# A gMLP block with one gelu per row tile, norms in place in three groups, a padded output projection, and outputs three tiles behind the gates

## The chip, the cores and the metric

The kernel runs on one core of a Trainium2 chip. The metric is the device time of one execution in microseconds (us), lower is better. TensorE is PE here, VectorE DVE, ScalarE ACT, GpSimd POOL, SyncE SP. SP, ACT and POOL also issue DMA transfers, each from its own queue, in the order of its instructions.

## The reference

Two layers run twice: a recurrent memory attention (A) and a gMLP (B), each behind a layer norm and a residual. Only B is changed. S is 2048 rows, D 512, F 1376, Fh 688.

```python
def _B_ref(x, w_in, w_sp, b_sp, w_out):
    z = _gelu(jnp.einsum('bsd,df->bsf', x, w_in))
    z1 = z[..., :Fh].copy()
    z2 = _layernorm(z[..., Fh:], axis=-1)
    g = jnp.einsum('ts,bsf->btf', w_sp, z2) + b_sp[None, :, None]
    return jnp.einsum('bsf,fd->bsd', z1 * g, w_out)
x = x + _A_ref(_layernorm(x, axis=-1), A_mem0, A_Wq, A_Wk, A_Wv, A_Wo, A_seg_len)
x = x + _B_ref(_layernorm(x, axis=-1), B_w_in, B_w_sp, B_b_sp, B_w_out)
```

The last two lines stand twice in the reference. Every gate row needs all 2048 rows of the normalised z2, so all of the projection comes before the first complete gate.

## The kernel before, in words

The program is A, B, A, B in time; the two B parts are called block 0 and block 1. A runs 64 segments of 32 rows, one after the other, and is not touched except in two places named below.

B (`b_block`, from line 227) works on 16 row tiles of 128 rows, in three stages.

**Projection.** `project` (line 261) takes the transposed input rows of one tile, runs twelve matmuls into `pz` (three PSUM banks, two buffers), then two gelus on ACT: the half to be normalised goes to an f32 tile `z2` (four buffers), the other half to `z1` in bf16. DVE takes statistics of `z2` (lines 273 to 275). After every second tile `norms` (line 277) computes the reciprocal roots of the two tiles on DVE, a chain of twelve small instructions in `_rstd_dve`, and ACT writes the normalised tiles to `z2n` (line 290), one pair behind the projection. The input rows come through `load_rows` (line 159), a DMA transpose on SP of two tiles at a time.

The last four row tiles of A (12 to 15) are not summed and normalised when B begins. `late_load` (line 253) loads their residual rows and A's output, POOL adds them (line 213) and stores them to `xd`; their statistics and norms go with the groups of tiles 5 and 7 on DVE (line 223), POOL stores the result to `xb_d`, and SP's transposes for tiles 12 to 15 read it. Their buffers are borrowed: one is a buffer of the spatial weights (`wspL`).

**Gates.** For each output tile t, `gate` runs 32 matmuls over the 16 source tiles into `pg`; `product` (line 335) adds the bias and multiplies by `z1` on DVE into `u`, whose 688 columns are padded to 768 by zeros; a DMA transpose on SP turns `u` into `uT`. The spatial weights `wspT` have three buffers: `product(t)` issues the load of t + 3, ahead of the transpose of `u` on SP's queue, and it waits until gate t has read its buffer.

**Outputs.** `finish` (line 357) runs six matmuls against `w_out`, in chunks of 128 rows and one of 48 (`FCH`), adds the residual on DVE into `xo` (one buffer), and stores it. In block 0 the statistics and reciprocal root of the output rows follow on DVE and ACT, for the next A. `finish(t - 2)` stands in the middle of gate t; the last tile is turned by PE and ACT (`turn_u`, line 349).

PE, DVE, ACT and, in B, SP run in the order of the code (`manual_schedule`, line 241); POOL's order is chosen by the framework. PE's order at the end of B is:

```python
for t in range(2, NT):
    gate(t, range(0, 10))
    finish(t - 2)
    gate(t, range(10, NT))
    product(t)
finish(NT - 2)
turn_u(NT - 1)
finish(NT - 1)
```

In A, `pads_of` splits some matmuls of a segment in two, so that each segment holds a whole number of pages of 256 PE instructions; `FILL_AHEAD` tells it how many stand before the first segment.

Of the kernel before, what the change touches and what calls it, by code (L numbers as in the profile page):

```python
# [14 lines left out]
P = 128  # L15
DM = 512
# [12 lines left out]
FILL_AHEAD = ((0, 0, 0, 106), (0, 0, 0, 94))  # L29
FCH = [(0, 128), (128, 128), (256, 128), (384, 128), (512, 128), (640, 48)]  # L30
# [137 lines left out]
class _Rows:  # L168
# [33 lines left out]
    def y_load(self, tb, first, eng, x=None, o=None):  # L202
        if x is None:
            x = self.pool.tile([P, DM], F32, name="y_x")[:]
            o = self.pool.tile([P, DM], F32, name="y_o")[:]
        x = x[:, 0:DM // 2].bitcast(BF16) if first else x
        eng.dma_start(x, (self.x_in if first else self.xd)[tb * P:(tb + 1) * P, :])
        eng.dma_start(o, self.o_d[M + tb * P:M + (tb + 1) * P, :])
        self.y[tb] = (o, x)

# [8 lines left out]
    def y_norm(self, tb, mean, rstd, store):  # L219

        o, _ = self.y.pop(tb)
        xn = self.pool.tile([P, DM], BF16, name="ln_xn", bufs=2)
        self.nc.vector.tensor_scalar(out=_nat(xn[:]), in0=_perm(o), scalar1=mean, scalar2=rstd, op0=ALU.subtract, op1=ALU.mult)
        store.dma_start(self.xb_d[tb * P:(tb + 1) * P, :], xn[:])


def b_block(tc, c, rows, front, xd, MV_out, RS_out, w_sp, w_out, S, first, out_final=None):
# [4 lines left out]
    with ExitStack() as ctx:  # L232
        mid = ctx.enter_context(tc.tile_pool(name="b_mid", bufs=1))
# [4 lines left out]
        ps_pool = ctx.enter_context(tc.tile_pool(name="b_ps", bufs=1, space=PSUM))  # L238
        big = _Tagged(ps_pool, "big", 2)
        one = _Tagged(ps_pool, "one", 2)  # L240
        ctx.enter_context(tc.manual_schedule(engines=ORDERED | {mybir.EngineType.SP}))

        w_in_sb = front.w_in_sb
        z1 = mid.tile([P, NT, FH], BF16, name="z1")
        z2n = mid.tile([P, NT, FH], BF16, name="z2n")
        w_out_sb = mid.tile([P, 6, DM], BF16, name="w_out_sb")
        xt, z2, wsp, mv, rs, nb = {}, {}, {}, {}, {}, {}
# [5 lines left out]
        def late_load(tb, x=None, o=None):  # L253
            rows.y_load(tb, first, nc.gpsimd, x=x, o=o)
            rows.y_add(tb, first, nc.gpsimd, nc.gpsimd)

        def load_wsp(t):
            wsp[t] = wsp_pool.tile([P, NT, P], BF16, name="wspT", tag="wspT")
            nc.sync.dma_start_transpose(out=wsp[t][:], in_=w_sp[t * P:(t + 1) * P, :].rearrange("t (st s) -> t st s", s=P))

        def project(tt):
            pz = big.tile([P, 1536], F32, name="pz")
            xnT = front.xnT[tt // 2][:, :, P * (tt % 2):P * (tt % 2) + P]
            for c0, c1 in ((0, 512), (512, 1024), (1024, FF)):
                for kt in range(KT):
                    nc.tensor.matmul(pz[:, c0:c1], lhsT=xnT[:, kt, :], rhs=w_in_sb[:, kt, c0:c1], start=(kt == 0), stop=(kt == KT - 1))  # L266
            z2[tt] = zp.tile([P, FH], F32, name="z2", bufs=4)
            nc.scalar.activation(out=z2[tt][:], in_=pz[:, 0:FH], func=ACT.Gelu_apprx_tanh)
            nc.scalar.activation(out=z1[:, tt, :], in_=pz[:, FH:FF], func=ACT.Gelu_apprx_tanh)
            if tt % 2 == 0:  # L270
                mv[tt // 2] = zp.tile([P, 4, 2], F32, name="mv")
            st = zp.tile([P, 2, nc.vector.BN_STATS_DIM], F32, name="bnst2")
            nc.vector.bn_stats(out=st[:, 0, :], in_=z2[tt][:, 0:344])
            nc.vector.bn_stats(out=st[:, 1, :], in_=z2[tt][:, 344:FH])
            nc.vector.bn_aggr(out=mv[tt // 2][:, tt % 2, :], in_=st[:])

        def norms(q, late):

            n = 4 if late else 2
            for k, tb in enumerate(late):  # L280
                rows.y_stats(tb, mv[q][:, 2 + k, :])
            rs[q] = zp.tile([P, 4], F32, name="rs")
            nb[q] = zp.tile([P, 2], F32, name="nb")
            _rstd_dve(nc, zp, rs[q][:, 0:n], mv[q][:, 0:n, 1], n)
            nc.vector.scalar_tensor_tensor(out=nb[q][:], in0=mv[q][:, 0:2, 0], scalar=-1.0, in1=rs[q][:, 0:2], op0=ALU.mult, op1=ALU.mult)
            for k, tb in enumerate(late):
                rows.y_norm(tb, mv[q][:, 2 + k, 0:1], rs[q][:, 2 + k:3 + k], nc.gpsimd)

        def normalise(tt):
            nc.scalar.activation(out=z2n[:, tt, :], in_=z2.pop(tt)[:], func=ACT.Identity, bias=nb[tt // 2][:, tt % 2:tt % 2 + 1],  # L290
                                 scale=rs[tt // 2][:, tt % 2:tt % 2 + 1])

        nc.gpsimd.dma_start(w_out_sb[:, 0:5, :], w_out[0:640, :].rearrange("(fc p) d -> p fc d", p=P))
        nc.gpsimd.dma_start(w_out_sb[0:48, 5, :], w_out[640:688, :])
        late_load(NT - 4)
        late_load(NT - 3, gp.tile([P, DM], F32, name="xs", bufs=3)[:], gp.tile([P, DM], F32, name="xo", bufs=1)[:])
        late_load(NT - 2, *(gp.tile([P, DM], F32, name="xs", bufs=3)[:] for _ in range(2)))
        wl = wsp_pool.tile([P, 2, DM], F32, name="wspL", tag="wspT")
        late_load(NT - 1, wl[:, 0, :], wl[:, 1, :])
        for tt in range(NT):  # L300
            project(tt)
            if tt in (7, 9, 11):
                load_wsp((tt - 7) // 2)
            if tt == 14:
                load_x(0)
            if tt % 2 == 1:
                if tt // 2 + 3 < NT // 2:
                    front.load_rows(tt // 2 + 3)
                norms(tt // 2, {5: (NT - 4, NT - 3), 7: (NT - 2, NT - 1)}.get(tt, ()))
                if tt > 1:  # L310
                    normalise(tt - 3)
                    normalise(tt - 2)
        normalise(NT - 2)
        normalise(NT - 1)

        zctx.close()
        up = ctx.enter_context(tc.tile_pool(name="b_u", bufs=2))

# [8 lines left out]
        def gate(t, sts):  # L327
            if sts[0] == 0:
                pg[t] = big.tile([P, 3, 512], F32, name="pg")
            for st in sts:  # L330
                for k in range(2):
                    nc.tensor.matmul(pg[t][:, k, 0:344], lhsT=wsp[t][:, st, :], rhs=z2n[:, st, 344 * k:344 * k + 344],  # L332
                                     start=(st == 0), stop=(st == NT - 1))

        def product(t):
            del wsp[t]
            if t + 3 < NT:
                load_wsp(t + 3)
            u[t] = us[t % 2]
            nc.vector.scalar_tensor_tensor(out=u[t][:, 0:FH].rearrange("p (k f) -> p k f", k=2), in0=pg.pop(t)[:, 0:2, 0:344],  # L340
                                           scalar=c["bsp"][:, t:t + 1], in1=z1[:, t, :].rearrange("p (k f) -> p k f", k=2),
                                           op0=ALU.add, op1=ALU.mult)
            if t + 1 < NT:
                load_x(t + 1)

                uT[t] = up.tile([P, 6, P], BF16, name="uT")
                nc.sync.dma_start_transpose(out=uT[t][:], in_=u[t][:].rearrange("t (fc s) -> t fc s", s=P))

        def turn_u(t):
            pT = one.tile([P, 1024], BF16, name="pT")  # L350
            for fc, (f0, fsz) in enumerate(FCH):
                nc.tensor.transpose(pT[0:fsz, fc * P:(fc + 1) * P], u[t][:, f0:f0 + fsz], ident_bf[:])
            uT[t] = up.tile([P, 6, P], BF16, name="uT")
            nc.scalar.copy(uT[t][:, 0:5, :].rearrange("p fc r -> p (fc r)"), pT[:, 0:640])
            nc.scalar.copy(uT[t][0:48, 5, :], pT[0:48, 640:768])

        def finish(t):
            py = one.tile([P, DM], F32, name="py")
            for fc, (f0, fsz) in enumerate(FCH):
                nc.tensor.matmul(py[:], lhsT=uT[t][0:fsz, fc, :], rhs=w_out_sb[0:fsz, fc, :], start=(fc == 0), stop=(fc == 5))  # L360
# [16 lines left out]
        gate(0, range(0, NT - 2))  # L377
        gate(1, range(0, NT - 2))
        gate(0, range(NT - 2, NT))
        product(0)  # L380
        gate(1, range(NT - 2, NT))
        product(1)
        for t in range(2, NT):
            gate(t, range(0, 10))
            finish(t - 2)
            gate(t, range(10, NT))
            product(t)
        finish(NT - 2)
        turn_u(NT - 1)
# [89 lines left out]
def a_block(tc, c, rows, front, MV_in, RS_in, MV_out, RS_out, wqkv, Wo, S, first):  # L479
# [6 lines left out]
    with ExitStack() as ctx:  # L486
# [383 lines left out]
        for s in range(NSEG):  # L870
# [21 lines left out]
            def tail():  # L892
# [11 lines left out]
                if due and (j4 != 3 or tb + 2 >= NB):  # L904
                    ys.append(due.pop(0))
                    rows.y_load(ys[0], first, nc.sync)
# [51 lines left out]
```

## Time and profile before

| what | us |
|---|---|
| median of 3 runs (1819.06 to 1823.71) | 1821.11 |
| the profiled execution, its own time | 1841.74 |
| its span on the core | 1840.0 |
| PE busy, of the span | 1729.5 (94%) |
| PE's weight loads | 1277.5 (69%) |
| DVE busy | 1172.4 (64%) |
| ACT busy | 1130.6 (61%) |
| POOL busy | 136.6 (7%) |
| block 0: first projection matmul to last output matmul | 776.87 to about 933.4 |
| block 1: the same | 1683.36 to about 1836.5 |

Times below are from the start of the profiled execution's span. The profiled execution is 20.6 us longer than the median of the plain runs, so differences are taken within it and then carried over to the median. A row of the timeline gives the start, the length, the engine, the line, the operation, output and inputs, shapes, and in brackets the idle time before it with what ended that. PE is matmuls, PEld the weight loads that run beside them; SPq, ACTq and POOLq are DMA instructions on those engines' queues.

### The profile page before, as it was taken

The page shows a single profiled execution, that of the slowest core. Times are in us where ns is not written, and L with a number is a line of the kernel's source. Part 1 is how long each engine was busy: PE and PEld are TensorE (multiplying, and loading weights), DVE is VectorE, ACT ScalarE, POOL GpSimd, SP SyncE. Part 2 cuts the span into 40 slices and gives each one's busy share as a digit, 9 for nine tenths or more (in the row PEclk, how much of TensorE's full clock was granted, in tenths as well). Part 3 has the DMA queues.
Part 4 walks back from the last instruction along what each step waited for, and adds up shares of the span by engine and source line. Part 5 has one row for each costly group of instructions (what it writes and reads, how often), then busy time and mean ns, then how long its engine had stood idle before and what let it go on. Part 6 is the DMA issues. An engine that isn't in the chain of part 4 may idle for free.

```text
span 1840.0 us, 109962 instructions
## 1 busy us (share of the span) xinstructions
PE 1729.5 (94%) x51154; PEld 1277.5 (69%) x51178; DVE 1172.4 (64%) x2956; ACT 1130.6 (61%) x2330; POOL 136.6 (7%) x289
## 2 busy tenths in 40 slices
PE   2999999999999999888979999999999999998898
PEld 1777777777777777645547777777777777775455
DVE  1666666677767766583446666666766776665622
ACT  1777777777777777571037777777777777765500
POOL 5000000000000000122010000000000000003000
PEclk8999999999999999999989999999999999999999
DMA  9100000021002112359840000001200120125576
GB/s 347 56 23 19 18 23 19 19 80 34 21 25 81 35 30 42 92 141 191 192 126 22 22 22 23 22 22 45 82 27 23 48 86 26 36 62 153 114 172 132
DMA packets 189331, 126.81 MB, mean 69 GB/s; under 512 B 135896, under 2 KB 164328, under 8 KB 188872
## 3 DMA queue, kind: packets, MB, share of 16 engines
q1 hardware_dynamic: 167016, 71.01, 16.7%
q0 software_dynamic: 10560, 34.07, 5.6%
q10 hardware_dynamic: 11296, 14.70, 2.7%
q8 instruction: 400, 6.55, 1.5%
q14 instruction: 59, 0.48, 0.1%
HBM read 59.29 MB, written 33.56 MB: 50 GB/s over the span
## 4 chain that ended last, share of the span: by engine, by line
PE 87%; issue 4%; DMA 3%; DVE 3%; ACT 1%; POOL 1%; SPq 0%; ACTq 0%; POOLq 0%; DVEq 0%
PE psm L544 13%; PE pw L602 13%; PE psV L544 13%; PE psm L719 12%; PE psb L544 10%; PE pg L332 8%; PE psS L743 4%; PE psO L769 4%; PE pwB L616 3%; PE py L360 3%; PE psD L824 2%; PE psM L815 1%; PE pz L266 1%; DMA Wo_sb<-in_A_Wo_dram 1%; DMA uT<-u 1%
## 5 line engine op out<-in xcount | busy, mean ns | idle before, releaser
L544 PEld LDWEIGHTS <-hA 128*32 128x32 bf16 x11102 | 361.5, 96 | 165.2 <-DVE hA L660 53.4
L544 PE MATMUL psV<-Wv_sb,hA 128*32 128x256 bf16 (+1 forms) x5880 | 288.1, 315 | 0.6 <-issue 0.2
L602 PE MATMUL pw<-Wo_sb,uT 128*32 128x128 bf16 x16640 | 269.6, 220 | 14.8 <-issue 8.1
L602 PEld LDWEIGHTS <-uT 128*32 128x32 bf16 x16640 | 238.6, 97 | 61.6 <-DVE uT L836 42.5
L706 ACT CAST rows<-psm 128x512 bf16<-128x512 f32 x256 | 149.8, 585 | 146.8 <-PE psm L544 146.8
L719 PEld LDWEIGHTS <-hA 128*32 128x32 bf16 x8192 | 237.8, 97 | 1.3 <-issue 0.5
L783 DVE TENSOR_TENSOR uT<-psO,Rt 128x384 bf16<-128x384 f32 x256 | 140.7, 550 | 100.5 <-ACT Rt L842 100.5
L722 ACT CAST rows<-psm 128x256 bf16<-128x256 f32 x512 | 191.2, 374 | 17.6 <-PE psm L719 0.3
L750 ACT ACTIVATE E<-psS 128x448 bf16<-128x448 f32 x256 | 126.3, 541 | 117.2 <-PE psS L743 117.2
L836 DVE TENSOR_TENSOR uT<-psO,Rm 128x128 bf16<-128x128 f32 x256 | 62.5, 286 | 174.8 <-PE psO L769 174.8
L544 PE MATMUL psm<-Wk_sb,hA 128*32 128x256 bf16 (+1 forms) x3158 | 151.9, 308 | 10.3 <-issue 8.9
L842 ACT ACTIVATE Rt<-Rt 128x512 f32<-128x512 f32 x256 | 157.4, 629 | 4.0
L332 PE MATMUL pg<-z2n,wspT 128*128 128x344 bf16 x1024 | 156.4, 311 | 1.0 <-DVE u L340 1.0
L544 PE MATMUL psm<-Wq_sb,hA 128*32 128x512 bf16 x2064 | 135.8, 384 | 10.2 <-DVE hA L660 8.8
L719 PE MATMUL psm<-Wq_sb,hA 128*32 128x256 bf16 x4096 | 138.5, 273 | 0.0
L719 PE MATMUL psm<-Wk_sb,hA 128*32 128x256 bf16 x4096 | 138.0, 273 | 0.0
L332 PEld LDWEIGHTS <-wspT 128*128 128x128 bf16 x1024 | 98.4, 98 | 55.6 <-issue 8.2
L544 PEld LDWEIGHTS <-hB 128*32 128x32 bf16 x3072 | 91.8, 98 | 62.7 <-DVE hB L559 25.3
L753 DVE TENSOR_TENSOR E<-E,maskN 128x448 bf16<-128x448 bf16 x256 | 104.2, 408 | 39.3 <-ACT E L750 37.7
L834 ACT ACTIVATE Rt<-psD 128x1024 f32<-128x1024 f32 x128 | 128.8, 1006 | 0.0
L710 DVE STREAM_TRANSPOSE QQ<-rows 128x512 bf16<-128x512 bf16 x128 | 88.9, 695 | 45.5 <-ACT rows L706 45.5
L710 DVE STREAM_TRANSPOSE KA<-rows 128x512 bf16<-128x512 bf16 x128 | 90.6, 708 | 38.3 <-ACT rows L706 37.8
(151 smaller groups left out, 2690.6 us busy)
## 6 DMA issues: line engine op xcount, KB each, us to landing
Wo_sb<-in_A_Wo_dram POOLq DMA_DIRECT2D x8, 1024.0 KB, 13.3
xs<-xd ACTq DMA_DIRECT2D x32, 256.0 KB
o_d<-o_sb SPq DMA_DIRECT2D x126, 64.0 KB
y_o<-o_d SPq DMA_DIRECT2D x24, 256.0 KB
xd<-y_o SPq DMA_DIRECT2D x22, 256.0 KB
Wq_sb<-in_A_Wq_dram POOLq DMA_DIRECT2D x8, 512.0 KB, 7.8
Wk_sb<-in_A_Wk_dram POOLq DMA_DIRECT2D x8, 512.0 KB, 11.1
Wv_sb<-in_A_Wv_dram POOLq DMA_DIRECT2D x8, 512.0 KB, 10.9
```

The lines of the kernel that those rows point to most:

```text
L332: nc.tensor.matmul(pg[t][:, k, 0:344], lhsT=wsp[t][:, st, :], rhs=z2n[:, st, 344 * k:344 * k + 344], start=(st == 0), stop=(st == NT - 1))
L544: nc.tensor.matmul(o, lhsT=lhs(kt, cg), rhs=r, start=(kt == 0 and a == 0), stop=(kt == KT - 1 or halved > 0), tile_position=(0, 32 * cg), ...
L602: nc.tensor.matmul(po[32 * cg:32 * cg + 32, 0:128], lhsT=lhs[:, n, :], rhs=wo_rhs(h, cg), start=(h == 0), stop=(h == H - 1), tile_position ...
L706: nc.scalar.copy(r[:], ps[:])
L710: nc.vector.transpose(out=QQ[:, j % 2, :, 0:32] if j < 2 else KA[:, j % 2], in_=r[:])
L719: nc.tensor.matmul(ps[32 * cg:32 * cg + 32, 0:256].rearrange("p (i c) -> p i c", i=2), lhsT=hA_cur[:, kt, :], rhs=qk_rhs(j, kt, cg)[:, 2 * ...
L722: nc.scalar.copy(r[:, 256 * a:256 * a + 256], ps[:, 0:256])
L750: nc.scalar.activation(out=E[:, r], in_=pS, func=ACT.Exp, scale=scale)
L753: nc.vector.tensor_tensor(out=E[:, r], in0=E[:, r], in1=maskN[:, j4, :].unsqueeze(1).to_broadcast([P, 4, 112]), op=ALU.mult)
L783: nc.vector.tensor_tensor(out=hview(uT_nxt[:], r, 8, 32), in0=oview(r, 8, 32), in1=r_view(r)[:, :, :, 0:24], op=ALU.mult)
L834: nc.scalar.activation(out=Rt[:], in_=psD[:], func=ACT.Ln)
L842: nc.scalar.activation(out=rt, in_=rt, func=ACT.Exp, scale=-1.0)
```

## The change

One gelu per tile writes all 1376 columns in bf16 to one array z, which is split in two tiles of 9 and 7 row tiles; `z1`, `z2` and `z2n` go. Statistics are taken from the bf16 values. The norms overwrite z in place, in three groups (0 to 3 with the four late rows, 4 to 9, 10 to 15): tiles 0 to 5 on ACT behind the gelus of 10 to 15, tiles 6 to 9 and 10 to 15 on DVE. The late rows are summed on DVE after tile 3; two of their norms stay on DVE, two go to ACT after tile 8. `w_out` is zero-padded, and the six chunks are all 128 rows. The code loads `w_out` at tile 11, and the third `w_sp` at tile 10 rather than 11. In the gate stage PSUM holds three gates of two banks each; the first ten source tiles of three gates run first, and outputs stand three tiles behind. Residual rows are loaded later. `y_load` returns the second load as a function to be called.

```diff
-FILL_AHEAD = ((0, 0, 0, 106), (0, 0, 0, 94))
-FCH = [(0, 128), (128, 128), (256, 128), (384, 128), (512, 128), (640, 48)]
+FILL_AHEAD = ((0, 0, 0, 106), (0, 0, 0, 88))
...
-    def y_norm(self, tb, mean, rstd, store):
+    def y_norm(self, tb, mean, rstd, store, shift=None):
...
+        if shift is not None:
+            self.nc.scalar.activation(out=_nat(xn[:]), in_=_perm(o), func=ACT.Identity, bias=shift, scale=rstd)
+        else:
+            self.nc.vector.tensor_scalar(out=_nat(xn[:]), in0=_perm(o), scalar1=mean, scalar2=rstd, op0=ALU.subtract, op1=ALU.mult)
...
+        zs = [ctx.enter_context(tc.tile_pool(name=f"b_z{n}", bufs=1)).tile([P, n, FF], BF16, name=f"z{n}") for n in (9, NT - 9)]
...
-            z2[tt] = zp.tile([P, FH], F32, name="z2", bufs=4)
-            nc.scalar.activation(out=z2[tt][:], in_=pz[:, 0:FH], func=ACT.Gelu_apprx_tanh)
-            nc.scalar.activation(out=z1[:, tt, :], in_=pz[:, FH:FF], func=ACT.Gelu_apprx_tanh)
...
+            nc.scalar.activation(out=z(tt), in_=pz[:, 0:FF], func=ACT.Gelu_apprx_tanh)
...
+        def normalise(*tts, dve=False):
+            for tt in tts:
+                mean, rstd, shift = scalars(tt)
+                if dve:
+                    nc.vector.tensor_scalar(out=z(tt, 0, FH), in0=z(tt, 0, FH), scalar1=mean, scalar2=rstd, op0=ALU.subtract, op1=ALU.mult)
+                else:
+                    nc.scalar.activation(out=z(tt, 0, FH), in_=z(tt, 0, FH), func=ACT.Identity, bias=shift, scale=rstd)
+
+        def late_sum(k):
+            rows.y_add(NT - 4 + k, first, nc.vector, nc.gpsimd)
+            rows.y_stats(NT - 4 + k, slot(("row", k)))
+
+        def late_norm(k, dve=False):
+            mean, rstd, shift = scalars(("row", k))
+            rows.y_norm(NT - 4 + k, mean, rstd, nc.gpsimd, shift=None if dve else shift)
+
+        GROUPS = ((0, 1, 2, 3) + tuple(("row", k) for k in range(4)), tuple(range(4, 10)), tuple(range(10, NT)))
...
+        nc.gpsimd.memset(w_out_sb[:, 5, :], 0.0)
         for tt in range(NT):
             project(tt)
...
+            if tt % 2 == 1 and tt // 2 + 3 < NT // 2:
+                front.load_rows(tt // 2 + 3)
+            if tt in (7, 9, 10):
+                load_wsp((7, 9, 10).index(tt))
+            if tt == 11:
+                nc.gpsimd.dma_start(w_out_sb[:, 0:5, :], w_out[0:640, :].rearrange("(fc p) d -> p fc d", p=P))
+                nc.gpsimd.dma_start(w_out_sb[0:48, 5, :], w_out[640:688, :])
+            if tt == 3:
+                for k in range(4):
+                    late_sum(k)
+                norms(GROUPS[0])
+                late_norm(0, dve=True)
+                late_norm(1, dve=True)
+            elif tt == 8:
+                late_norm(2)
+                late_norm(3)
+            elif tt == 9:
+                norms(GROUPS[1])
+                normalise(6, 7, 8, 9, dve=True)
+            elif tt > 9:
+                normalise(tt - 10)
+        norms(GROUPS[2])
+        normalise(*GROUPS[2], dve=True)
...
+        two = _Tagged(ps_pool, "two", 3)
+        one = _Tagged(ps_pool, "one", 2)
...
+            uT[t] = up.tile([P, 6, P], BF16, name="uT", bufs=3)
...
+            if t > 0:
+                load_x(t - 1)
...
-            for fc, (f0, fsz) in enumerate(FCH):
-                nc.tensor.matmul(py[:], lhsT=uT[t][0:fsz, fc, :], rhs=w_out_sb[0:fsz, fc, :], start=(fc == 0), stop=(fc == 5))
+            for fc in range(6):
+                nc.tensor.matmul(py[:], lhsT=uT[t][:, fc, :], rhs=w_out_sb[:, fc, :], start=(fc == 0), stop=(fc == 5))
...
+        for t in range(3):
+            gate(t, range(0, 10))
+        for t in range(3):
+            gate(t, range(10, NT))
+            product(t)
+        for t in range(3, NT):
+            gate(t, range(0, 10))
+            finish(t - 3)
+            gate(t, range(10, NT))
+            product(t)
+        load_x(NT - 1)
+        finish(NT - 3)
+        turn_u(NT - 1)
         finish(NT - 2)
-        turn_u(NT - 1)
         finish(NT - 1)
```

## The prediction, as it stands on record

> **What bounds the kernel now.** I read the page's busy table and chain of waits (PE 87% of the chain), then cut the two gMLP blocks out with the table by stretches: projection, opening of the gates, steady gates, tail.
>
> ```profile
> core 0: us, PE busy (x) PEld busy (x) DVE busy (x) ACT busy (x) POOL busy (x), PEclk, DMA share, GB/s
> 776.87:822.70 45.83, 37.72 (x188) 18.73 (x192) 37.55 (x139) 31.89 (x45) 14.62 (x23) 1.00 0.63 157
> 833.40:926.20 92.80, 87.03 (x522) 50.48 (x528) 35.06 (x58) 6.47 (x26) 11.37 (x18) 0.98 0.91 191
> 926.20:934.40 8.20, 4.79 (x19) 1.54 (x18) 3.58 (x8) 1.73 (x6) 0.97 (x2) 0.79 0.17 64
> 1683.36:1729.90 46.54, 40.75 (x188) 19.64 (x192) 38.19 (x143) 32.09 (x45) 15.20 (x23) 0.93 0.64 163
> ```
>
> The columns are the stretch, its length, and the busy time of PE, its loads, DVE, ACT and POOL, then clock, DMA share and GB/s: projection, steady gates and tail of block 0, projection of block 1. PE is the busiest in each, yet in both projections 6 to 8 us short of full, with DVE next at 37.6; only the steady gates are close to full. Sixteen projected tiles take 45.8 and 46.5 us; two neighbouring tiles run 787.13 to 791.78, so 2.32 us each and 37.1 in all: 9 us a block are not PE's. PE's waits in block 0 name them:
>
> ```profile
> PE pz L266 <- ACT z L269: 7.9, 5, 2.5
> PE py L360 <- DMA uT<-u: 5.5, 2, 3.0
> PE py L360 <- ACT uT L354: 2.3, 1, 2.3
> PE pg L332 <- DVE u L340: 0.5, 1, 0.5
> ```
>
> Each row is a wait of PE: for whom, total, times, longest. In block 1 the same list gives 5.6, 3.2, 1.4, 0.5. ACT is not the cause of the first: the timeline has it waiting for DVE's nb, and DVE is stretched to 2.86 us on an instruction that takes 0.16 elsewhere, exactly while POOL's adds (L213) run; read from top to bottom, each row releases the next:
>
> ```profile
> 791.60 2.86 DVE L132 SCALAR_TENSOR_TENSOR ny<-nq,nb 128x2 f32<-128x2 f32 x1
> 792.16 1.17 POOL L213 TENSOR_TENSOR xs<-xs 128x512 f32<-128x512 f32 x1
> 795.87 1.81 ACT L290 ACTIVATE z2n<-z,nb,rs 128x688 bf16<-128x688 f32 x2 [2.45 <-DVE nb L285]
> 798.99 4.81 PE L266 MATMUL pz<-front 128*128 128x512 bf16 x23 [2.40 <-ACT z L269]
> ```
>
> One steady gate period, 887.51 to 893.68, is 6.17 us:
>
> ```profile
> 887.51 4.84 PE L332 MATMUL pg<-z2n,wspT 128*128 128x344 bf16 x32
> 892.05 0.89 PEld L360 LDWEIGHTS <-uT 128*128 128x128 bf16 x5
> 893.36 0.09 PEld L360 LDWEIGHTS <-uT 48*128 48x128 bf16 x1 [0.42 <-issue]
> 893.68 4.49 PEld L332 LDWEIGHTS <-wspT 128*128 128x128 bf16 x32 [0.23 <-issue]
> ```
>
> The 32 gate matmuls cost 4.59 (their loads run gapless from 887.51 to 892.0; 344 columns at the 2.4 per ns that 512 columns in 213 ns show), six outputs at 0.213 cost 1.28: 5.87. The missing 0.30 stands around the 48-row chunk (the brackets are idle time before its load and before the next gate's), and nowhere else: the step from the gates into the outputs, 892.0 to 892.05, has none.
>
> **The change part by part.** T0 is the projection's last matmul, g the last gate's. Waits in the changed kernel are taken from its built instruction order.
>
> *Projection, before 45.8/46.5.* One gelu of 1376: the PSUM-reading ACT rows give 374, 585 and 1006 ns for 256, 512 and 1024 columns, so 0.163 + 0.824 ns each, 1.30 us (bounds: 1.28, the two starts 0.64 apart now; 1.48, two of 738 ns). With a normalise (0.91 from L290, now six on ACT instead of sixteen) ACT needs 2.2 a tile, below PE's 2.32. DVE sheds five of eight reciprocal-root chains (2.35 us each) and its POOL stretches, gains four sums (L213 on DVE 0.69). Late:
> - The gelu table load now waits for tile 0's matmuls: 1.28 + 1.30 after 2.32 + 0.2 holds tile 2 for 0.6.
> - Transposes of row tiles 12 and 13 wait for DVE: stats of tile 3 at +12.5, four sums with stats at 1.65 (6.6), chain 2.35, two norms 1.0: +22.5; store and landing 2.5 (803.1 to 805.64 now), transpose 4.4 (813.52 to 817.96): +29.4. Tile 12 is due at 28.4. Stall 1.0.
> - Late norms 2 and 3 sit on ACT's queue ahead of gelu 9 and wait for the store of the buffer that norm 0 filled: about +25 to +26. Gelu 9 then ends at +27.2 and holds tile 11 by 1.1; this is the same microsecond as the stall above. 0.3 more for norm 3's transpose, queued on SP behind w_sp 0.
> 37.1 + 0.6 + 1.0 + 0.3 = 39.0. **Gain 6.8 and 7.5.** Bounds 1 and 9. The in-place bf16 norms on DVE have no row: nearest L223, 0.54 for 512, so 0.73 (below: 0.16, the smallest DVE row). Six after a chain end near T0 + 10.5; their chunks are read from T0 + 10.2 to 11.6 in step: hidden, by about 1.
>
> *w_out.* POOL's order is not held by hand, and the build puts memset (0.48 from L553), 0.87 and 0.54 of issue ahead of the last o_sb store: earlier than now, not later. POOL idles there (31.3 us before 769.78) and the four y_o loads lose 1.4 us of issue before them. Cost 0; if the memset waited past 769.8, y_o and all that follows it would be late by as much.
>
> *Gates, T0 to g, before 103.8/101.6 (822.70 to 926.46, 1729.90 to 1831.53).* Gone: padding 14 x 0.30 = 4.2; one finish moved behind g, 1.6; waits for uT 5.5/3.2 and u 0.5; half clock after the wait, 1.8 (five outputs in 2.37 for 1.35, a gate round 5.6 for 4.84). Sum 13.6/11.3. Added: the first gate waits for the last gelu (built order), 0.2 + 1.30 + 0.05 = 1.55. Gate 3 is now reached 3.4 us (two half gates of 1.72) after gate 0 frees its w_sp buffer; load 3 was issued at 831.68 and its 290 GB/s ended near 836.1, so 4.6: wait 1.2. Queued behind these are only PE's own gates. Three tiles behind, uT 0 arrives at T0 + 18.6, its finish at 19.5: hidden by 0.9. Other: 0.3 clock, 0.5 for DMA in block 0, where the share reaches 0.91 and the period shrinks 5%. **Gain 10.1 and 8.3**; bounds 4 and 12.
>
> *Tail, behind g.* turn_u stands behind finish 13, its copy (one of 768, 0.80, for two) beside finish 14. But xo has one buffer, so each add waits for the store before it: at most 2.53 (store 925.37, add 927.90 unheld), taken 2.3. Three adds: g + 1.5, 4.5, 7.6, last store g + 8.2 where it was 5.7 (1837.22): block 1 **loses 2.5** (bounds -3.2 and 0.3, were stores never in the way). In block 0 the A block's copies queue on ACT behind the last rstd, g + 10.2 for 9.9, but two of its products are then already made: **gain 0.8** (bounds -1 and 2.4).
>
> *Fill 94 to 88* pads segment 0 with three matmul pairs; the built order has block 1's first wo pass at PE instruction 51,803 for 51,804, so page boundaries stay in place: 0.
>
> Sum 6.8 + 7.5 + 10.1 + 8.3 + 0.8 - 2.5 = 31.0. On the profiled execution: 1841.74 - 31 = 1810.7. The runs' median is 20.6 below it; the same 31 from 1821.11: **1790**.
>
> **Two rules against the rows.** The Trainium skill, "TensorE: Matmul & The Clock Gate", section "Why this matters for your kernels": a K=32 matmul takes the time of K=128. By the rule padding 48 rows to 128 gains nothing; by the row it gains 0.30 x 32 = 9.6 over the kernel. The row decides: both gaps are at the chunk in every period. The same section asks for no PE gap above about 3 us; shorter ones would be free. Rows: after gaps of 2.25 (1705.37), 2.47 (1719.01) and 3.2 (1746.28) loads stand 0.43 apart for some 3 us. By the rule, removing a wait gives the wait; by the rows about 1.6 more each, some 5 in block 1, contained in the 46.5 and the 1.8 above. Rows again.
>
> **Rivals.**
> 1. *The late rows hold the projection* (16%): DVE's sums wait for y_o or norm 3's transpose comes 3 to 4 us late. For: tile 14 has under 1 us of slack, ACT's gelus queue behind two DMA waits. Against: POOL issues y_o earlier. Projection 43: 31 - 8 = 23, **1798**.
> 2. *The padding gives nothing and DMA holds block 0's gates* (10%): for, the rule and the share of 0.91, 1.13 near 850 to 865. Against: uT now has 5.87 us more patience. 31 - 9.6 - 4 = 17, **1804**.
> 3. *The waits I added are not there* (12%): store and w_sp landings shorter, late rows in time: +2.4 + 2 + 2.5: **1784**.
> 4. *Slower: instruction pages* (3%). At L602 PE pauses on issue 50 matmuls into the pass (1.21 at 767.89). If block 1's one-instruction shift put such a pause elsewhere in each of its 64 segments, 0.49 us a segment eats the gain; at 0.7, **1835**. For: such pauses cost 8.1 us in 19 places of pw's waits now. Against: the shift is one instruction, and from block 0 to block 1 there is one already.
> 5. *Nothing moves* (1%): gains given back in A, **1821**.
> Mine has the remaining 58%, its own range 1785 to 1795. The range 1782 to 1802 takes in cases 1 and 3 and about half of 2's spread. Faster by over 0.3% (5.5 us, about what this kernel's measurement tells from no change): 0.95; within: 0.02; slower: 0.03.
>
> **What would show it.** Projections of about 39 us, no POOL add, no DVE stretch; loads of the sixth uT chunk 0.2 after the fifth and a period of 5.87; one wait each for the last gelu and for w_sp 3 of 1 to 2 us; no uT wait; last store 8 us behind g. Wrong if the period stays 6.17, projections stay over 43, or A of block 1 changes by more than 2 us.

## The result, and the profile after

The changed kernel takes 1796.04 us (median of 4 runs, 1794.31 to 1805.57), the kernel before 1822.41 beside it: ratio 0.9864, 95% interval 0.9829 to 0.9899, so 26 us (18 to 31) faster, where 31 was forecast. A second set of runs gave 0.9851 (0.9805 to 0.9898).

The profiled execution took 1805.57, 36.2 less than the one of before. Not all of that is the change's: the first projection matmul stands at 767.29, not 776.87, and nothing ahead of it is edited. So the two kernels are compared by stages of the gMLP blocks. Projection is the first projection matmul to the last one's end; gates from there to the last gate matmul's end; tail 0 from there to A's first `pw` matmul; tail 1 from there to the end of the span. Each kernel was profiled twice; "forecast" is the first profile of before less the prediction's gains.

| us | before | before, again | forecast | after | after, again |
|---|---|---|---|---|---|
| projection, block 0 | 45.9 | 46.1 | 39.1 | 40.6 | 39.1 |
| projection, block 1 | 46.7 | 47.7 | 39.2 | 40.1 | 39.1 |
| gates, block 0 | 103.6 | 103.6 | 93.5 | 98.6 | 94.2 |
| gates, block 1 | 101.4 | 100.9 | 93.1 | 94.2 | 94.3 |
| tail 0 | 25.0 | 24.4 | 24.2 | 24.7 | 24.3 |
| tail 1 | 8.6 | 8.6 | 11.1 | 10.4 | 10.4 |
| sum of the blocks | 331.2 | 331.3 | 300.2 | 308.5 | 301.4 |
| A of block 1 (no gMLP) | 731.9 | 724.9 | | 728.1 | 724.0 |

The blocks gained 22.7 us in the first pair of profiles and 29.9 in the second. From the table by stretches of the first changed profile, with columns as in the prediction: block 0's projection up to the first gate and its steady gates, then the same of block 1.

```profile
767.29:809.42 42.13, 37.83 (x192) 18.69 (x192) 28.97 (x91) 28.22 (x27) 8.82 (x17) 1.00 0.66 155
824.70:906.57 81.87, 79.38 (x495) 48.93 (x496) 33.06 (x54) 6.03 (x25) 11.20 (x18) 0.98 1.04 203
1659.22:1700.82 41.60, 37.83 (x192) 18.68 (x192) 28.99 (x91) 28.19 (x27) 9.29 (x18) 1.00 0.75 173
1716.00:1793.63 77.63, 77.63 (x495) 48.40 (x496) 21.13 (x26) 0.00 (x0) 0.00 (x0) 1.00 0.81 179
```

DVE has fallen from 37.6 to 29 in a projection, and PE is busy 37.8 of 42 (1.4 of the rest stands ahead of the first gate). The last row is PE without any gap. The same 495 matmuls of block 0 take 4.2 us more, at a DMA share of 1.04. PE's waits from 800 to 930 name most of it (five of seven rows; `psb` belongs to the next A):

```profile
PE pg L360 <- DMA wspT<-in_B_w_sp_dram: 3.6, 2, 2.5
PE psb L571 <- DVE xo L395: 2.3, 1, 2.3
PE pz L266 <- DMA front<-xb_d: 1.7, 1, 1.7
PE pg L360 <- ACT z L267: 1.4, 1, 1.4
PE py L386 <- ACT uT L381: 1.4, 1, 1.4
```

No wait for a transfer into uT is left; the last row is the copy of the last tile on ACT, 2.3 before the change. The waits for w_sp, for the input rows (`front`) and for the last gelu are new. All were forecast, except the w_sp wait of 2.5, late in the gates. That wait and 3.41 us of half clock behind it (868.83 to 872.24) are the 4.2.

A steady period in block 1, 1779.80 to 1785.76, is 5.96 us, where it was 6.17:

```profile
1779.80 4.83 PE L360 MATMUL pg<-z,wspT 128*128 128x344 bf16 x32
1784.32 1.11 PEld L386 LDWEIGHTS <-uT 128*128 128x128 bf16 x6
1785.54 4.69 PEld L360 LDWEIGHTS <-wspT 128*128 128x128 bf16 x32
1785.76 4.83 PE L360 MATMUL pg<-z,wspT 128*128 128x344 bf16 x32
```

The six output loads stand in one row: the gap of 0.42 ahead of the sixth and the one of 0.23 behind it are gone. At the end two adds wait for the single `xo` to be stored:

```profile
1797.52 0.69 DVE L391 TENSOR_TENSOR xo<-py,xs 128x512 bf16<-128x512 f32 x1 [1.86 <-DMA out_dram<-xo]
1800.05 0.69 DVE L391 TENSOR_TENSOR xo<-py,xs 128x512 bf16<-128x512 f32 x1 [1.84 <-DMA out_dram<-xo]
```

### The profile page after: what moved, and what is told of

Same layout as the page of the kernel before. It is cut to its first block, busy times and chain, and to the rows that moved or that the text cites. A ratio compares the mean times of both kernels' runs of the same rounds, so it can differ in the third digit from the quotient of the medians.

```text
span 1803.9 us, 109796 instructions
## 1 busy us (share of the span) xinstructions
PE 1707.5 (95%) x51181; PEld 1274.2 (71%) x51181; DVE 1156.7 (64%) x2850; ACT 1115.7 (62%) x2280; POOL 128.2 (7%) x283
## 4 chain that ended last, share of the span: by engine, by line
PE 87%; DMA 5%; issue 3%; DVE 2%; POOL 1%; ACT 1%; POOLq 0%; SPq 0%; ACTq 0%; DVEq 0%
PE psm L571 14%; PE psV L571 13%; PE pw L629 13%; PE psm L746 12%; PE psb L571 9%; PE pg L360 8%; PE psS L770 5%; PE psO L796 4%; PE pwB L643 3%; PE psD L851 2%; PE py L386 2%; PE psM L842 1%; DMA wspT<-in_B_w_sp_dram 1%; PE pz L266 1%; DMA Wo_sb<-in_A_Wo_dram 1%
## 5 line engine op out<-in xcount | busy, mean ns | idle before, releaser
L360 PE MATMUL pg<-z,wspT 128*128 128x344 bf16 x1024 | 155.9, 311 | 7.4 <-DMA wspT<-in_B_w_sp_dram 4.6
L746 PE MATMUL psm<-Wq_sb,hA 128*32 128x256 bf16 x4096 | 143.3, 273 | 0.0
L746 PE MATMUL psm<-Wk_sb,hA 128*32 128x256 bf16 x4096 | 142.7, 273 | 0.0
L571 PEld LDWEIGHTS <-hB 128*32 128x32 bf16 x3072 | 86.2, 97 | 64.4 <-DVE hB L586 25.3
## 6 DMA issues: line engine op xcount, KB each, us to landing
Wk_sb<-in_A_Wk_dram POOLq DMA_DIRECT2D x8, 512.0 KB, 11.1
```

Of the source, the lines that this page charges most:

```text
L571: nc.tensor.matmul(o, lhsT=lhs(kt, cg), rhs=r, start=(kt == 0 and a == 0), stop=(kt == KT - 1 or halved > 0), tile_position=(0, 32 * cg), ...
L746: nc.tensor.matmul(ps[32 * cg:32 * cg + 32, 0:256].rearrange("p (i c) -> p i c", i=2), lhsT=hA_cur[:, kt, :], rhs=qk_rhs(j, kt, cg)[:, 2 * ...
```

## The experiments

Plain runs of one kernel spread over 10 us and more, and A of block 1 lies between 722.9 and 731.9 in the fourteen profiles of this study. Differences of a few us are therefore read from the blocks' stages; ratios are to the kernel before, run beside each.

### The changed kernel again

> The changed kernel once more, unedited, to see which of its stage times repeat. Theory: everything in the two gMLP blocks repeats within 0.5 us (first projection matmul to first gate 42.1 and 41.6, gates 97.2 and 92.8, with one wait of about 2.5 us for w_sp late in block 0), and only A, made of 128 segments with scattered PE stalls of 0.1 to 0.6 us each, moves by several us from execution to execution; ratio to the kernel before 0.985 to 0.989. Rival: the 8 us that the blocks' stages lack against the prediction are chance of one profiled execution; then the w_sp wait of 2.5 or the 1.7 wait at tile 14 is missing here and the blocks are 4 us or more shorter.

Its blocks take 301.4. The early w_sp wait is there in both blocks, the late one is not, and tile 14 waits 0.2 and 0.4 for its rows:

```profile
PE pg L360 <- DMA wspT<-in_B_w_sp_dram: 1.0, 1, 1.0
PE pz L266 <- DMA front<-xb_d: 0.2, 1, 0.2
```

The rival holds: of the 7 us by which the first profile is longer, 4.4 stand in block 0's gates and 2.5 in the projections, and the waits that are shorter or missing here are nearly all for transfers. In the seven profiles with three w_sp buffers and outputs three tiles behind, the late w_sp wait stands in the first alone.

### The kernel before again

> The kernel before once more, unedited, for the spread of its own stages, as the changed kernel's two profiles differ by 7 us inside block 0's projection and gates. Theory: its blocks' stages (projections 45.9 and 46.7, gates 103.6 and 101.4, tails 25.0 and 8.6) repeat within 1 us except the waits for a DMA (uT 5.5 and 3.2), which move by up to 3; A of block 1 (731.9) comes out between 724 and 732. Rival: the blocks of the first profile were themselves slow by chance; then they come out 4 us or more shorter and the change is worth less than 26.

The sum repeats within 0.1 us; the uT waits are 5.2 and 2.7. The change is worth 22.7 to 29.9 us in the blocks.

### No padding

```diff
-            for fc in range(6):
-                nc.tensor.matmul(py[:], lhsT=uT[t][:, fc, :], rhs=w_out_sb[:, fc, :], ...)
+            for fc in range(6):
+                n = 128 if fc < 5 else 48
+                nc.tensor.matmul(py[:], lhsT=uT[t][0:n, fc, :], rhs=w_out_sb[0:n, fc, :], ...)
```

> The changed kernel with the last output chunk back at 48 rows. By the row of the kernel before (0.30 us around each 48-row chunk) 32 x 0.30 = 9.6 us slower than the changed kernel, steady period 6.26; by the steady period of the changed kernel (5.96 against 6.17) 32 x 0.21 = 6.7 us slower, period 6.17; by the skill's rule that a short contraction costs the same as a full one, no difference, period 5.96.

Gates 97.1 and 97.1 for 94.2 and 94.3: 2.85 a block over 13 outputs, 0.22 each; ratio 0.9892 (0.9841 to 0.9943). The loads near the end of block 1, with the gaps back:

```profile
1773.66 0.89 PEld L387 LDWEIGHTS <-uT 128*128 128x128 bf16 x5
1774.97 0.09 PEld L387 LDWEIGHTS <-uT 48*128 48x128 bf16 x1 [0.42 <-issue]
1775.29 4.49 PEld L360 LDWEIGHTS <-wspT 128*128 128x128 bf16 x32 [0.23 <-issue]
1779.83 0.89 PEld L387 LDWEIGHTS <-uT 128*128 128x128 bf16 x5
```

The period is 6.17. Neither 0.30 nor zero, as the skill's rule on one matmul would have it, is right: with the gaps gone, 32 gate loads span 4.69, not 4.49, so a part is given back there. Tail 0 is 28.5 here, with 10.2 us of it at a granted clock of 0.5, where the changed kernel's two profiles have none.

### Padding alone, in the kernel before

```diff
-FCH = [..., (512, 128), (640, 48)]
+FCH = [..., (512, 128), (640, 128)]
...
+        nc.gpsimd.memset(w_out_sb[:, 5, :], 0.0)
...
-            nc.scalar.copy(uT[t][0:48, 5, :], pT[0:48, 640:768])
+            nc.scalar.copy(uT[t][:, 5, :], pT[:, 640:768])
```

> The kernel before with only the padding: the sixth chunk of w_out filled with zeros to 128 rows. From the changed kernel without padding (gates 2.85 a block longer over 13 outputs, 0.22 each): 32 x 0.22 = 7 us faster than the kernel before, period 5.95. The prediction's row said 0.30 x 32 = 9.6 and 5.87; the skill's rule says 0 and 6.17. It can be eaten partly where uT comes too late anyway: waits for uT up by up to 0.2 a tile.

Ratio 0.9979 (0.9955 to 1.0003): some 4 us with an interval from 8 to none, where 7 were expected. In its one profile the blocks take 333.3, 2 us longer than before. Block 1's gates fell to 98.5, 2.4 to 2.9 less, with a wait for uT of 3.2 as before, but block 0's rose from 103.6 to 109.2: PE waited 6.92 us for a uT. SP's queue and PE's rows around it:

```profile
850.96 7.18 SPq L259 DMA_TRANSPOSE wspT<-in_B_w_sp_dram  x1
858.25 1.23 SPq L348 DMA_TRANSPOSE uT<-u  x1
858.83 2.74 PE L361 MATMUL py<-w_out_sb,uT 128*128 128x512 bf16 x6 [6.92 <-DMA uT<-u]
861.37 6.18 PE L333 MATMUL pg<-z2n,wspT 128*128 128x344 bf16 x32
```

The issue of one w_sp load took 7.18 us on SP, and the transpose of u stood behind it; the gate after the wait then took 6.18 for 4.83, with a granted clock of 0.50 until 864.12. Whether the faster gates brought this wait, or that execution's transfers did, is not shown: issues of 5.0 and 5.7 us stand in block 0 of the kernel before too.

### Two tiles behind

```diff
-        for t in range(3):
+        for t in range(2):
             gate(t, range(0, 10))
...
-            finish(t - 3)
+            finish(t - 2)
...
-        finish(NT - 3)
         turn_u(NT - 1)
```

> The changed kernel with outputs two tiles behind the gates instead of three (two gates opened first, the last product turned before finish 14). The prediction's terms: waits for uT come back (up to 5.5 in block 0 and 3.2 in block 1, with up to 1.8 of half clock behind each group), one finish moves back in front of the last gate's end and its 1.6 is lost to nobody; the wait of gate 3 for w_sp (1.1) goes: 4 to 8 us slower than the changed kernel. Rival, a saturated DMA in block 0: there the wait of 2.5 for w_sp is merely replaced by one of about 3 for uT, block 0's gates stay within 1.5 us, and the whole is at most 3 us slower.

Gates 101.8 and 96.9, 7.6 and 2.6 longer than in the changed kernel; tail 0 1.2 longer, tail 1 1.0 shorter: 10.4 us in the blocks (311.8) against the changed kernel's second profile, 3.3 against its first. Ratio 0.9883 (0.9835 to 0.9931), which the runs alone don't tell from the changed kernel's 0.9851. Waits in block 0:

```profile
PE py L386 <- DMA uT<-u: 5.3, 3, 2.5
PE pT L380 <- DVE u L368: 2.5, 1, 2.5
```

In block 1 the same two waits are 2.4 and 1.0. The waits for uT are about those of the kernel before (5.5 and 3.2), so the third tile of distance is worth what the removed waits said. The second row, the last tile's transpose on PE waiting for DVE, is what the expectation lacked. The distance doesn't only trade uT for w_sp.

### Two xo buffers

```diff
...
-            xo = gp.tile([P, DM], F32, name="xo", bufs=1)
+            xo = gp.tile([P, DM], F32, name="xo", bufs=2)
```

and the same at the two other places where `xo` is made.

> The changed kernel with two xo buffers. Theory one, the single xo buffer makes the late wait for w_sp in block 0 (an add waits 7.7 us for the store before it, and product and transposes stand behind it on DVE): the w_sp wait of 2.5 and its half clock go, the add waits of the tail go, block 0's gates 4 us shorter, last store 2 us nearer to the last gate in block 1 and 2 in block 0: 6 to 8 us faster than the changed kernel. Theory two, the DMA is full between 836 and 873 whatever DVE does: the add waits go, the w_sp wait stays within 1 us of 2.5, and only the tails gain, 2 to 4 us.

Gates 94.4 and 94.4, unchanged; tail 0 22.8 and tail 1 8.5, 1.5 and 1.9 shorter; blocks 298.3. Ratio 0.9866 (0.9821 to 0.9912), not told apart from the changed kernel by the runs, as A took 731.1. The adds now wait for PE:

```profile
1796.73 0.69 DVE L391 TENSOR_TENSOR xo<-py,xs 128x512 bf16<-128x512 f32 x1 [0.94 <-PE py L386]
1798.63 0.69 DVE L391 TENSOR_TENSOR xo<-py,xs 128x512 bf16<-128x512 f32 x1 [1.20 <-PE py L386]
```

The tail's loss is the single buffer's. Of the late w_sp wait it tells nothing, since the changed kernel's second profile didn't have that wait either.

### Sums on DVE, in the kernel before

```diff
-            rows.y_add(tb, first, nc.gpsimd, nc.gpsimd)
...
+            if tt == 3:
+                for k in range(4):
+                    rows.y_add(NT - 4 + k, first, nc.vector, nc.gpsimd)
```

> The kernel before with the four late sums on DVE after tile 3 in place of POOL, nothing else. Theory: POOL's adds stretch DVE's small instructions (0.16 to 2.86 us) and with them the normalises and gelus; without them PE's waits for gelus shrink from 7.9 and 5.6 to 3 to 4, so each projection takes 42 to 43 us in place of 45.9 and 46.7: 6 to 8 us faster. Rival: the projection is held by ACT's sixteen pairs of gelus and normalises (2.39 us a tile against PE's 2.32) and the eight reciprocal-root chains whoever sums: gain under 2 us, and the waits stay above 6.

Projections 45.0 and 44.7: 0.9 to 1.1 us shorter in block 0 and 2.0 to 3.0 in block 1, not 4. Even that is partly the clock: block 0 has one stretch of 3.41 us at half clock in its projection here and none before, block 1 none here and two before. The blocks take 321.7, 9.6 less than before, but 4.5 of it is in block 0's gates, which the edit doesn't touch and where PE waited 2.4 us for uT instead of 5.5. The ratio is 0.9979 (0.9954 to 1.0003). No DVE instruction of block 0's projection takes over 0.75 us any more, and ACT still waits for `nb`, the shift that a normalise adds, which DVE's chain makes last. ACT's row in block 0's projection, first the kernel before, then this one:

```profile
ACT z2n L290 <- DVE nb L285: 8.8, 5, 2.9
```

```profile
ACT z2n L289 <- DVE nb L284: 6.6, 4, 2.9
```

In block 1 it is 8.0 and 7.7. A normalise in ACT's queue waits for the pair's reciprocal-root chain on DVE, and the next gelus stand behind it. POOL's adds made that chain later, but the two longest waits left (2.0 and 2.9 in either block) come where DVE has the statistics of two late rows ahead of the chain.

### Two gelus, in the changed kernel

```diff
-            nc.scalar.activation(out=z(tt), in_=pz[:, 0:FF], func=ACT.Gelu_apprx_tanh)
+            nc.scalar.activation(out=z(tt, 0, FH), in_=pz[:, 0:FH], func=ACT.Gelu_apprx_tanh)
+            nc.scalar.activation(out=z(tt, FH), in_=pz[:, FH:FF], func=ACT.Gelu_apprx_tanh)
```

> The changed kernel with two gelus of 688 per tile in place of one of 1376. If the groups are what counts: two gelus take 0.63 + 0.74 = 1.37 on ACT in place of 1.31, with a normalise of 0.95 exactly PE's 2.32 from tile 10 on, so projections within 1 us of 39.1 and the blocks within 2 us. Rival, the single gelu is worth most of the projection's gain: projections 42 or more.

Projections 38.2 and 38.1, about 1 us **shorter** than with one gelu; blocks 298.9, ratio 0.9835 (0.9808 to 0.9862). PE waits for gelus once for 0.5, where the changed kernel waits twice for 1.1 in all. One gelu per tile is no part of the projection's gain.

### Norms in pairs, in the changed kernel

```diff
-        GROUPS = ((0, 1, 2, 3) + tuple(("row", k) for k in range(4)), tuple(range(4, 10)), tuple(range(10, NT)))
+        GROUPS = (tuple(("row", k) for k in range(4)),) + tuple((q, q + 1) for q in range(0, NT, 2))
...
+            if tt % 2 == 1:
+                norms(GROUPS[1 + tt // 2])
+                if tt > 1:
+                    normalise(tt - 3, tt - 2)
...
```

> The changed kernel with norms in pairs again: after every second tile a chain of reciprocal roots on DVE, and ACT normalises one pair behind, all sixteen tiles on ACT; one gelu per tile, late sums on DVE and everything else as changed. Theory after the run with sums on DVE alone: the projection was held by the pairs, whose normalises stand in ACT's queue waiting for a chain on DVE with the next gelus behind them; projections go back from 39.1 to 42 to 45 us. Rival: the single gelu is what freed ACT (1.30 + 0.95 under PE's 2.32); projections stay under 41, and only the last pair's normalise is late for the gates, 1 to 3 us.

Projections 48.4 and 47.7, longer even than before the change; ratio 0.9929 (0.9902 to 0.9956); blocks 321.4.

```profile
798.79 1.81 ACT L298 ACTIVATE z<-z,nb,rs 128x688 bf16<-128x688 bf16 x2 [8.53 <-DVE nb L284]
800.50 2.50 ACT L267 ACTIVATE z<-pz 128x1376 bf16<-128x1376 f32 x2
801.85 6.82 PE L266 MATMUL pz<-front 128*128 128x512 bf16 x24 [8.30 <-ACT z L267]
```

Again a normalise waits for `nb`, here behind the four sums and their chain on DVE, and two gelus and PE behind it. In the changed kernel's projection (second profile, block 0) the list of ACT's waits has none for `nb`; a late row's norm waits once, 1.2. But this is one wait, and the 24 matmuls behind it take 6.82 for 4.81, at half clock until 805.96. Without the 8.3 and the 2.0 block 0's projection would be 38.1. So, by subtraction and not by a run, pairs cost nothing apart from the place where the late rows' work stands ahead of a chain that ACT waits for. Pairs with that work put elsewhere were not tried.

### The fill as before

```diff
-FILL_AHEAD = ((0, 0, 0, 106), (0, 0, 0, 88))
+FILL_AHEAD = ((0, 0, 0, 106), (0, 0, 0, 94))
```

> The changed kernel with the fill of block 1's first segment planned for 94 instructions, as before the change, so that all PE instructions of block 1's A stand six pairs away from their place. Theory: A of block 1 stays within its spread over identical code (723 to 732), stages of the blocks unchanged. Rival four of the prediction, an instruction page boundary in a bad place of each segment: A of block 1 longer by 31 us or more (0.49 a segment).

A of block 1 took 723.0, among the shortest; ratio 0.9834 (0.9803 to 0.9865). Such a shift does nothing here.

### The added waits taken away

```diff
-        wsp_pool = ctx.enter_context(tc.tile_pool(name="b_wsp", bufs=3))
+        wsp_pool = ctx.enter_context(tc.tile_pool(name="b_wsp", bufs=4))
+        two0 = _Tagged(ctx.enter_context(tc.tile_pool(name="b_ps0", bufs=1, space=PSUM)), "two0", 1)
...
-                normalise(6, 7, 8, 9, dve=True)
-            elif tt > 9:
+                normalise(5, 6, 7, 8, 9, dve=True)
+            elif 9 < tt < 15:
...
-        two = _Tagged(ps_pool, "two", 3)
+        two = _Tagged(ps_pool, "two", 2)
...
-                pg[t] = two.tile([P, 2, 512], F32, name="pg")
+                pg[t] = (two0 if t % 3 == 0 else two).tile([P, 2, 512], F32, name="pg")
```

with the two `xo` buffers.

> The changed kernel with two xo buffers, four w_sp buffers, the first gate's PSUM in two banks that the projection doesn't use, and tile 5 normalised on DVE beside 6 to 9 (ACT normalises five). Theory: each of the waits that the change added goes: last gelu 1.4, w_sp 3 1.0, add waits 1.9 and 1.5; of the first, up to 1 us can stay as gate 0 reaches tile 4 or 10 before its norm is done. Blocks 298.3 (two xo buffers) minus 2 x (1.4 + 1.0) = 293.5, so 8 us under the changed kernel's 301.4. Rival: behind the removed wait the next one stands, z of the later tiles normalised after the last gelu; then T0 to last gate stays above 93.5 and the blocks above 297.

Gates 91.8 and 91.5, 2.4 and 2.8 less, tail 1 1.7 less; blocks 296.0. In the gates of block 0 PE waits for nothing; the opening is one run of 116 matmuls:

```profile
809.55 17.08 PE L361 MATMUL pg<-z,wspT 128*128 128x344 bf16 x116
826.47 1.46 PE L387 MATMUL py<-w_out_sb,uT 128*128 128x512 bf16 x5
```

1788.37 us beside 1829.79: ratio **0.9778 (0.9745 to 0.9811)**, faster than the kernel before, and in the blocks 5.4 us shorter than the changed one. Projection 0 stayed at 40.0 (tile 14's rows, 0.9 late), and A's opening lost 2.7 us on `issue` (1.6 in the changed kernel's second profile), so the forecast 293.5 was missed by 2.5.

### And the row transposes ahead of w_sp

The kernel of the last section with one more edit:

```diff
-            if tt in (7, 9, 10):
-                load_wsp((7, 9, 10).index(tt))
+            if tt in (9, 10, 11):
+                load_wsp((9, 10, 11).index(tt))
```

> The kernel with two xo and four w_sp buffers, free PSUM for the first gate and tile 5 on DVE, and beyond it w_sp loads 0 to 2 moved from tiles 7, 9, 10 to 9, 10, 11, so that the last transpose of input rows stands ahead of all of them on SP's queue. Theory: the wait of tile 14 for its rows (0.9 and 0.4; 1.7 in the first profile of the change) goes, projections 38.7 to 39.0 in both blocks, gates unchanged at 91.6: blocks 1 to 1.5 us under 296. Rival: w_sp 0 is then late for the first gate, which waits 1 us or more for it.

Projections 38.6 and 38.6; no wait for rows, none of the first gate. Blocks 293.9, the shortest; ratio 0.9792 (0.9764 to 0.9820), not told from the last kernel's by the runs. Block 0's gates are 92.9, with a wait in the middle of them in spite of the fourth w_sp buffer:

```profile
867.95 1.91 PE L361 MATMUL pg<-z,wspT 128*128 128x344 bf16 x12
871.08 3.09 PE L361 MATMUL pg<-z,wspT 128*128 128x344 bf16 x20 [1.22 <-DMA wspT<-in_B_w_sp_dram]
```

So a fourth buffer doesn't keep such a wait away, which leaves the transfers themselves: the two w_sp issues ahead of it on SP took 4.54 and 6.06 us. That the late w_sp wait of 2.5 in the changed kernel's first profile was of the same kind is likely, not shown.

## Why the prediction was right, step by step

- **Projection.** The size is right (39.1 in both blocks of the second profile, for 39.0). The forecast stalls of 0.6, 1.0 and 0.3 are 0.4, 0.7 and 0.2 in that profile's block 0, at tiles 2, 11 and 14. In the first profile tile 14 waited 1.7 in block 0, for its rows, and 1.4 in block 1; there the row names a gelu, but it is the one of tile 13, whose buffer tile 14 doesn't use, and the transpose of the rows was issued only 3.6 us earlier.
  Its cause is half right. "ACT is not the cause ...: the timeline has it waiting for DVE's nb" holds: that wait is 6.6 to 8.9 us in the three kernels with long projections where it was listed and absent from the changed kernel's short one. The stretch "exactly while POOL's adds (L213) run" is true of the rows, but taking the adds away gave only 1 to 3 us of 7. And the gelu, on which ACT's sum rests, gives nothing. What the waits point to is DVE's work on the late rows while a normalise stands in ACT's queue. The changed kernel does most of that work at tile 3, and ACT's first normalise stands behind the gelu of tile 10. The split between this, the larger groups and the normalises moved to DVE is open.
- **Padding.** 0.22 per output, not 0.30: "14 x 0.30 = 4.2" is 2.85 a block. This is the mis-sized term of the sum, and its reading "2.4 per ns that 512 columns in 213 ns show" is what failed. In the trace of the kernel before, matmuls of 512 columns start 216 ns apart and those of 344 columns 146, so 6 and 32 of them take 5.97 and not 5.87. That leaves 0.20 of the 6.17 for the gaps around the 48-row chunk, and the changed kernel's period is 5.96. The gates of the second profile lack 0.7 and 1.2 of their forecast, about 14 x 0.09.
  The rule of the Trainium skill ("TensorE: Matmul & The Clock Gate", "Why this matters for your kernels") that was weighed against the row is about a single matmul, and there the trace agrees: without the padding, an output matmul of 48 rows is recorded with 387 ns, one of 128 rows with 379. It doesn't give the price of a 48-row chunk in a stream of full ones, which by it would have been zero.
- **Waits for uT.** Right as a whole: two tiles behind costs 10.4 us in the blocks, 3.5 of it the last transpose's wait for DVE. The padding alone brought about 4 us of 7, with an interval down to none, and one late uT in its profile; whether a shorter period makes these waits longer, which a sum of separate terms can't foresee, is open.
- **Added waits.** The first gate waits 1.4 for the last gelu (1.55 forecast), gate 3 waits 1.0 to 1.1 for w_sp (1.2), the tail loses 1.8 (2.5); with all of them removed together, the time came back. All are there, so rival 3 falls. "0.5 for DMA in block 0" was too low for the first profile, where the w_sp wait and the slow loads behind it cost 4.4, and about right for the second: rival 2's transfers, in one execution of seven.
- **Half clock.** "By the rows about 1.6 more each, some 5 in block 1" is right. Up to the last gate, both profiles of the kernel before have three stretches of 3.41 us at a granted clock of 0.5 in block 1 and one in block 0, each of which can cost half its length, 1.7. The changed kernel has none but the one behind the late w_sp wait of its first profile. The 3 us that the same section of the skill names are no limit here: waits of 2.25 and 2.47 were followed by half clock, one of 2.98 was not; the last section says what tells them apart.
- **Fill.** 0, as forecast; rival 4 falls. The prediction's own sign of being wrong, a change of more than 2 us in A of block 1, was too fine: A changed by 3.8 in the first pair of profiles and by 0.9 in the second, but the kernel before differs from itself by 7.0.

Forecast and second profile agree to 1.2 us in the blocks (31.0 and 29.9), the first lacks 8.3. The runs' 26.4 lies between, and their interval, 18 to 31, holds both profiles' gains. A contributes nothing that its own spread doesn't cover.

## What to carry to other kernels

An operation in an in-order queue that waits for another engine's chain delays everything behind it. So first look at what the waiting engine waits for, and do the other engine's extra work where nothing in the queue waits for it, before making the first engine's work cheaper. Where a wait for a transfer is near and the transfer's time varies, give it more distance than its usual time asks for. To price a gap, take the pace of the stream around it from the start times in the trace, not from a rate. Profile an unedited kernel twice before explaining a difference of a few us, and compare by stages that the edit touches.

## What the hardware showed besides

**A long issue holds SP's queue.** The issue of a w_sp transpose on SP took 1.9 us at least and 2.7 in the median (block 0 of the last kernel). The longest one was 3.8 to 7.2 us in block 0 of the fourteen profiles and 3.0 to 4.3 in block 1; the 6.7 of the changed kernel's first profile came at a DMA share of 1.2. What is next on SP's queue waits behind it.

**Half clock follows a mostly idle step, not a long wait.** In every profile the granted clock changes only at moments that lie whole multiples of 3.41 us apart. Two stretches of such steps in the kernel before, with the columns of the prediction's first table:

```profile
1716.06:1719.47 3.41, 0.94 (x7) 0.42 (x5) 3.24 (x12) 3.41 (x5) 1.07 (x2) 1.00 0.98 182
1719.47:1722.88 3.41, 3.41 (x11) 1.33 (x10) 3.06 (x16) 2.27 (x4) 0.00 (x0) 0.50 0.39 77
862.73:866.14 3.41, 2.01 (x14) 1.13 (x12) 0.07 (x1) 0.00 (x0) 2.13 (x4) 1.00 1.19 113
866.14:869.55 3.41, 1.83 (x9) 0.91 (x11) 0.45 (x1) 0.00 (x0) 0.96 (x2) 1.00 1.16 235
869.55:872.96 3.41, 3.41 (x26) 2.26 (x24) 2.06 (x4) 0.50 (x2) 0.00 (x0) 1.00 1.25 235
```

A wait of 2.47 us, ending at 1719.01, falls into one step, PE is busy for 0.94 of it, and the next step has half the clock. A wait of 2.98 us, ending at 867.72, is divided over two steps, PE is busy for 2.01 and 1.83, and the clock stays. In the blocks of the fourteen profiles, tails included, there are 1237 whole steps at full clock. All 38 with more than 2.05 us idle on PE were followed by half clock, none of the 1182 with less than 1.69 was, and 5 of the 17 between. So a wait's place counts as well as its length.

**The same instructions vary.** The first 64 segments of A, the same instructions in both kernels, took 710.6 us from the first to the last in one profile of the kernel before and 702.0 in one of the changed; the kernel before took 700.6 in its other profile. The shortest segment is 10.79 in both of the first two; most others are longer by 0.1 to 1.5, and which ones changes from one profile to the next.
